# Pooled attention and token mixer: exponentials stored in pairs, value halves split over three matmuls, 22 heads with a column of ones

## Chip, cores and metric

One core of a Trainium2 chip runs the whole program. The metric is device time in microseconds (us) of one execution, from the median of several runs. The engines are TensorE (PE for its matmuls, PEld for its weight loads), VectorE (DVE), ScalarE (ACT), GpSimd (POOL) and SyncE (SP), which issues the transfers.

## What is computed

The input q, k, v has 4 batches of 8 heads, 1152 rows and 64 columns in float32. Attention comes first, with pairs of query rows averaged (576 queries); the heads are then put side by side (512 columns), and a mixer follows over the tokens and over the channels.

```python
q_pool = q.reshape(B, H, S // 2, 2, D).mean(axis=3)
scores = scale * np.matmul(q_pool, k.transpose(0, 1, 3, 2))
scores = scores - np.max(scores, axis=-1, keepdims=True)
attn = np.exp(scores)
attn = attn / (np.sum(attn, axis=-1, keepdims=True) + 1e-09)
x = heads_side_by_side(np.matmul(attn, v))          # 4 x 576 x 512
h = np.maximum(x.transpose(0, 2, 1) @ w_tok1, 0.0) @ w_tok2
u = x + h.transpose(0, 2, 1)
out = u + np.maximum(u @ w_ch1, 0.0) @ w_ch2
```

The mixer's weights come as float64 words and are made float32 on the chip. (The line with heads_side_by_side stands for a transpose and a reshape.)

## The kernel before

Every float32 number that goes into a matmul is split into a high half (rounded to the fast matmul type fp32r) and a low half (the rest), so a product takes two or three fp32r matmuls. The program is a list of steps, each with an engine, an estimated cost and a due time from the table DUE (in units of one step of the attention loop). Plan.run walks through the list and always takes the step that can start first by these estimates, the due time only deciding between equals. What comes out is a fixed order for each engine; on the chip the engines run these orders with semaphores, so a step that takes longer than its estimate delays what stands behind it on its engine.

The 32 heads follow each other (h in main, L757). A head has nine steps s (NK is 9), and each step handles two blocks of 128 keys by 288 queries: the four score matmuls (L781) go into one of two PSUM buffers "s"; ScalarE takes the exponentials of them twice, once in float32 into PF (L791, pf) and once rounded into ph (L794); the difference pl is made by GpSimd or VectorE (L798; both() leaves the choice to the planner, but the first four heads use GpSimd alone). The product with V (L823) adds up in the single PSUM buffer "o" over nine key blocks and is copied out by ScalarE into OT (L828) twice a head, for queries 0 to 287 and 288 to 575. V lies in VV as 64 columns of high half and 64 of low half (L638, L641).

The sum of the exponentials is made in one of two ways. In the heads of IN_PV (18 of 32) one column of VV is set to ones (L645), so that the matmuls of L823 give the sum as one more row; the column that is lost is kept in V0 (L643) and costs a third matmul with weights of one column. In the other 14 heads VectorE adds up the nine blocks of PF (L805), in three pieces of 96 queries for each half of the queries, six a head; the nine numbers that are added lie 288 elements apart.

finish (L832) turns the result to queries by columns and adds the two halves in one go: five plain float32 matmuls of OT with FOLD, two stacked identities (L845). In the 14 heads without ones, five more with a single column of ones add SUM over the partitions (L852). Then come the sum plus a small number (L857), its reciprocal (L859) and the product into U (L864, L867).

Ahead of a head's scores its row maxima are found by matmuls into a ring of three PSUM banks "r" (L717), each reduced by VectorE (L719). The ring also serves the transposes (L575, L601, the mixer's L991), finish and the token mixer (L898, L916). The token weights are narrowed from float64 words (L352 to L362, L513, L521, L523) in the second head, between the attention's steps; their temporaries lie in SBUF. The channel part (L1013, L1041) runs after all heads.

## Time and profile before

| | us |
|---|---|
| median of 3 runs | 947.64 |
| the three runs | 947.71, 941.20, 947.64 |
| span of the profiled execution (first to last instruction) | 940.4 |
| PE busy | 912.0 (97%) |
| PE weight loads busy | 837.5 (89%) |
| VectorE busy | 686.0 (73%) |
| ScalarE busy | 515.1 (55%) |
| GpSimd busy | 377.4 (40%) |
| mean granted TensorE clock | 0.990 |

The profiled execution's span is 0.8 us under the quickest of the timed runs; what lies around the span is thus taken as 0.8 us. The shares are means over the span: attention with the token mixer fills about the first 625 us, and the channel part the rest. The busy time of a matmul in the profile is its latency and overlaps with that of the next; the rate of a stream of matmuls is read from the chain that ended last, where each has only the time that it adds.

### The profile page before, as it was taken

What the parts mean: (1) busy time and instruction counts of PE and PEld (TensorE: products, weight loads), DVE (VectorE), ACT (ScalarE), POOL (GpSimd) and SP (SyncE); (2) the same over time, 40 slices, a digit from 0 to 9 for tenths busy, and PEclk for the clock granted to TensorE, in tenths of its full rate; (3) what the DMA queues carried; (4) which work ended last, traced back from release to release, by engine and by line L of the source; (5) the groups of instructions that cost most, each with busy time, mean ns of one, the idle gap of its engine ahead of it and who ended that gap; (6) DMA issues with size and microseconds to landing.
All of it is one profiled execution on the core that took longest, in us unless ns stands there. A gap on an engine that the chain in (4) does not pass through costs nothing.

```text
span 940.4 us, 15866 instructions
## 1 busy us (share of the span) xinstructions
PE 912.0 (97%) x5857; PEld 837.5 (89%) x5857; DVE 686.0 (73%) x1243; ACT 515.1 (55%) x1040; POOL 377.4 (40%) x342
## 2 busy tenths in 40 slices
PE   7999989999999999999999999999999999999997
PEld 5878879899999989899899999989999998999996
DVE  7887989899999999999999998998872222121311
ACT  3867857687787776776877776854431111111110
POOL 2788866576475574484664763400000000000000
PEclk9999979999999999999999999999999999999999
DMA  6984544537637536645564342034420101000001
GB/s 159 257 184 118 132 105 120 135 87 160 131 86 163 119 86 136 131 113 121 109 138 108 89 108 77 24 97 149 135 90 1 68 1 35 1 34 1 33 1 34
DMA packets 89685, 91.10 MB, mean 97 GB/s; under 512 B 43852, under 2 KB 68808, under 8 KB 89608
## 3 DMA queue, kind: packets, MB, share of 16 engines
q1 hardware_dynamic: 89608, 90.09, 40.4%
q8 instruction: 46, 0.75, 0.4%
q14 instruction: 31, 0.25, 0.1%
HBM read 43.25 MB, written 4.72 MB: 51 GB/s over the span
## 4 chain that ended last, share of the span: by engine, by line
PE 66%; DVE 2%; ACT 1%; DMA 0%; issue 0%; POOL 0%; DVEq 0%; POOLq 0%
PE r L1013 16%; PE s L1041 12%; PE o L823 11%; PE s L781 9%; PE r L717 4%; PE o L1041 3%; PE r L916 3%; PE r L845 2%; PE r L898 2%; PE r L852 1%; PE r L1041 1%; PE r L575 1%; PE r L991 1%; DVE mx L719 1%; DVE pl L798 1%; DMA vn<-in_v_dram 0%
## 5 line engine op out<-in xcount | busy, mean ns | idle before, releaser
L798 POOL TENSOR_TENSOR pl<-pf,ph 128x576 fp32r<-128x576 f32 x194 | 278.4, 1455 | 126.3 <-ACT ph L794 76.1
L791 ACT ACTIVATE pf<-s 128x576 f32<-128x576 f32 x288 | 189.1, 658 | 108.2 <-PE s L781 103.2
L719 DVE TENSOR_REDUCE mx<-r 128x1 f32<-128x384 f32 x384 | 198.4, 548 | 17.1 <-PE r L717 14.5
L794 ACT ACTIVATE ph<-s 128x576 fp32r<-128x576 f32 x288 | 188.9, 657 | 10.3 <-PE s L781 6.4
L781 PE MATMUL s<-qq,kk 128*128 128x288 f32 x574 | 167.6, 304 | 2.9 <-ACT ph L794 2.2
L781 PE MATMUL s<-q,k 65*128 65x288 f32 x576 | 165.5, 300 | 0.5 <-DMA q<-mt 0.2
L1021 DVE SCALAR_TENSOR_TENSOR h<-r,h 128x384 fp32r<-128x384 f32 x72 | 40.1, 556 | 166.9 <-ACT h L1019 166.9
L805 DVE TENSOR_REDUCE sum<-pf 128x96 f32<-128x864 f32 x84 | 146.4, 1750 | 0.2
L823 PE MATMUL o<-ph,vv 128*128 128x288 f32 x576 | 141.5, 306 | 0.2
L1019 ACT ACTIVATE h<-r 128x384 fp32r<-128x384 f32 x72 | 35.3, 491 | 193.5 <-PE r L1013 193.5
L717 PE MATMUL r<-kk,qq 128*128 128x384 f32 x372 | 127.7, 362 | 11.2 <-DVE mx L719 5.2
L823 PE MATMUL o<-pl,vv 128*128 128x288 f32 x576 | 135.5, 299 | 0.5 <-DVE pl L798 0.5
L1041 PE MATMUL s<-w,h 128*128 128x512 f32 x504 | 131.0, 394 | 0.0
L781 PEld LDWEIGHTS s<-qq,kk 128*128 128x128 f32 x574 | 109.4, 191 | 6.9 <-ACT ph L794 5.4
L781 PEld LDWEIGHTS s<-q,k 65*128 65x128 f32 x576 | 110.1, 191 | 1.6 <-issue 1.5
L1013 PE MATMUL r<-big,w 128*128 128x384 f32 x576 | 109.0, 337 | 0.0
L1041 PEld LDWEIGHTS s<-w,h 128*128 128x128 f32 x504 | 93.4, 188 | 16.6 <-DVE h L1021 0.2
L823 PEld LDWEIGHTS o<-pl,vv 128*128 128x128 f32 x576 | 98.2, 190 | 8.4 <-DVE pl L798 0.7
L1013 PEld LDWEIGHTS r<-big,w 128*128 128x128 f32 x576 | 101.8, 188 | 3.9 <-DVE h L1021 0.2
L823 PEld LDWEIGHTS o<-ph,vv 128*128 128x128 f32 x576 | 100.6, 192 | 2.9 <-ACT ot L828 2.1
L717 PEld LDWEIGHTS r<-kk,qq 128*128 128x128 f32 x372 | 69.8, 194 | 20.7 <-DVE mx L719 8.7
L798 DVE TENSOR_TENSOR pl<-pf,ph 128x576 fp32r<-128x576 f32 x94 | 76.6, 819 | 3.9 <-ACT ph L794 3.4
(134 smaller groups left out, 1273.4 us busy)
## 6 DMA issues: line engine op xcount, KB each, us to landing
raw<-in_moe_w_ch_dram SPq DMA_DIRECT2D x24, 512.0 KB
kk<-kh SPq DMA_DIRECT2D x32, 288.0 KB
kk<-kl SPq DMA_DIRECT2D x32, 288.0 KB
qq<-qh SPq DMA_DIRECT2D x64, 144.0 KB
vn<-in_v_dram SPq DMA_DIRECT2D x32, 288.0 KB
k<-kk SPq DMA_DIRECT2D x31, 288.0 KB
kn<-in_k_dram SPq DMA_DIRECT2D x30, 288.0 KB
qn<-in_q_dram SPq DMA_DIRECT2D x32, 256.0 KB
```

Source lines behind the costliest of these rows:

```text
L717: step(PE, mm(SP3), lambda ps=ps, w=w, x=x: te.matmul(at(ps)[:, 0:SP3], w, x, start=True, stop=True), t, read, [ps], [ps])
L719: step(DVE, dve(SP3), lambda ps=ps, m=m: ve.tensor_reduce(m, at(ps)[:, 0:SP3], axis=AX.X, op=ALU.max), t + due["max_of"], [ps], [key])
L781: te.matmul(at(st)[:, i, 0:HF], w[:, c * P:(c + 1) * P], x[:, fq * HF:(fq + 1) * HF], start=(n == 0), stop=(n == len(terms) - 1))
L791: step(ACT, act_ps(2 * HF), lambda pf=pf, st=st: sc.activation(pf, at(st)[:, :, 0:HF], AF.Exp, scale=ESC), t, [(st, 0), (st, 1)], [("pf", s)])
L794: step(ACT, act_ps(2 * HF), lambda ph=ph, st=st: sc.activation(at(ph), at(st)[:, :, 0:HF], AF.Exp, scale=ESC), t + due["p_hi"], [(st, 0), ...
L798: both(2 * HF, lambda e, pf=pf, ph=ph, pl=pl: e.tensor_sub(at(pl), pf, f(at(ph))), t + due["p_lo"], [("pf", s), ph], [pl], [pl], on=POOL i ...
L805: step(DVE, 65 + 1.83 * NK * HF // CUT, lambda fq=fq, cs=cs: ve.tensor_reduce(SUM[:, fq, cs], PF[:, fq * NK:(fq + 1) * NK, cs].rearrange(" ...
L823: lambda o=o, x=x, w=w, m=m, i=i, c=c, new=new, end=end: te.matmul(at(o)[0:m], w[:, c], at(x)[:, i], start=new, stop=end),
L1013: te.matmul(at(ps)[:, 0:GT], w[:, c], x[:, c], start=(c == 0 and n == 0), stop=(c == NC4 - 1 and n == 2))
L1019: step(ACT, act_ps(GT), lambda: sc.activation(at(h)[:, 0], at(ps)[:, 0:GT], AF.Relu), t, [ps], [h])
L1021: step(DVE, dve(GT), lambda: ve.scalar_tensor_tensor(out=at(h)[:, 1], in0=at(ps)[:, 0:GT], scalar=0.0, in1=f(at(h))[:, 0], op0=ALU.max, op ...
L1041: te.matmul(at(ps), a[:, x * P:(x + 1) * P], w, start=(fi == 0 and m == 0), stop=(fi == NF - 1 and m == 2))
```

## The change

- IN_PV grows from 18 to 22 heads, so 10 heads are left in which VectorE adds up the exponentials.
- VV gets 130 columns a block, with a lasting column of ones behind the second half. In the heads of IN_PV the low half of V comes first and the high half second, beside the ones. Three matmuls a block stay: ph with high half and ones (65 columns of weights), ph with the low half (64), pl with high half and ones (65), all into the same rows of "o". V0 and GpSimd's two small steps (L643, L645) go. OT then has 65 rows, with the two halves of V added already.
- In the other heads the two matmuls of 128 columns stay; ScalarE copies the lower rows of "o" to LOW, and VectorE adds them to the upper rows into OT. So "o" is free only after both.
- PF holds neighbouring blocks in pairs: the exponentials of a step are written with a step of two elements (8 bytes), read so by L798, and summed as ten blocks in five pairs, the tenth being zero.
- finish transposes OT (64 or 65 rows by 128 columns) instead of multiplying by FOLD. In the 10 heads without ones, SUM is transposed too (five of 128 by 128) into a second bank of the ring, and VectorE reduces it along the free axis (512 and 128 elements).
- The bits of the token weights are put together in a bank of the ring "r" in place of an SBUF temporary, and the low half is always made by VectorE.
- All numbers of DUE are new, and so the order on every engine can change. The estimate of GpSimd's cost rises a little, and the planner gives VectorE a step that both could do only when GpSimd would end 135 ns later (before 7.7).

```diff
-    "sum": -2.82,
+    "sum": -6.47,
...
-    "stay": 7.7,
+    "stay": 135.0,
...
+IN_PV = (0, 1, 2, 3, 4, 5, 7, 9, 11, 12, 13, 15, 16, 18, 19, 21, 22, 23, 25, 27, 28, 31)
...
-    IN_PV = (0, 1, 2, 3, *range(5, 32, 2))
...
-    FOLDS = 114
+    DT = D + 1
...
-        return 150 + 2.1 * n
+        return 175 + 2.1 * n
...
-    PF = fix.tile([P, 2 * NK, HF], F32, name="pf")
+    PF = fix.tile([P, 2, (NK + 1) // 2, HF, 2], F32, name="pf")
     SUM = fix.tile([P, 2, HF], F32, name="sum")
     REST = words(SUM).rearrange("p f x -> p (f x)")[:, 0:2 * J]
 
 
-    FOLD = many(fix, 2, [P, D + 1], F32, "fold")
+    LOW = fix.tile([D, SQ], F32, name="low")
...
-    VV = many(fix, 2, [P, NK, 2 * D], F32R, "vv")
-    V0 = many(fix, 2, [P, NK, 1], F32R, "v0")
+    VV = many(fix, 2, [P, NK, 2 * D + 2], F32R, "vv")
...
+    for i in range(2):
+        po.memset(f(VV[i])[:, :, P:P + 1], 1.0)
+        po.memset(OT[i], 0.0)
     ve.memset(f(QD[1]), 0.0)
+    po.memset(PF[:, :, NK // 2, :, 1], 0.0)
...
-                w, read = Buf("w"), [("raw", i, c), ("stage",), *(rest if (i, c) == (1, 4) else [])]
+                w, ps, read = Buf("w"), Buf("r"), [
+                    ("raw", i, c), ("stage",), *(rest if (i, c) == (1, 4) else [])]
 
                 def tmp(w=w, r=r, m=m):
                     return at(w)[r, 0:m]
 
-                def clamp(tmp=tmp):
-                    po.tensor_scalar(
-                        out=tmp(), in0=tmp(), scalar1=F64_LEAST, scalar2=F64_MOST,
-                        op0=ALU.max, op1=ALU.min)
-
-                for n, (eng, cost, fn) in enumerate(narrow(tmp, lambda w=words_[r, o]: w, m)):
-                    if n == 1:
-                        eng, cost, fn = POOL, 150 + 1.1 * m, clamp
-                    step(eng, cost, fn, t, read, [w], [w] if n == 0 else [], shared=eng == DVE)
-                step(ACT, act(m), lambda a=wh[r, o], w=tmp: sc.copy(a, w()), t,
-                     [w], [("w", i, c)])
-                both(m, lambda e, a=wl[r, o], w=tmp, d=f(wh)[r, o]: e.tensor_sub(a, w(), d), t,
-                     [w, ("w", i, c)], [("w", i, c)])
+                def low(ps=ps, r=r, m=m):
+                    return at(ps)[r, 0:m]
+
+                def raw_(k, words_=words_, r=r, o=o):
+                    return words_[r, o][:, :, k]
+
+                step(ACT, act(m), lambda raw_=raw_, tmp=tmp: sc.activation(
+                    tmp(), raw_(1).bitcast(F32), AF.Abs), t, read, [w], [w])
+                step(POOL, 150 + 1.1 * m, lambda tmp=tmp: po.tensor_scalar(
+                    out=tmp(), in0=tmp(), scalar1=F64_LEAST, scalar2=F64_MOST,
+                    op0=ALU.max, op1=ALU.min), t, [w], [w])
+                t2 = t + due["w_bits"]
+                step(DVE, dve(m), lambda tmp=tmp, low=low: ve.tensor_scalar(
+                    out=words(low()), in0=words(tmp()), scalar1=0x07FFFFFF, scalar2=3,
+                    op0=ALU.bitwise_and, op1=ALU.logical_shift_left), t2, [w], [ps], [ps])
+                step(DVE, dve(m), lambda raw_=raw_, low=low: ve.scalar_tensor_tensor(
+                    out=words(low()), in0=raw_(1), scalar=0xC0000000, in1=words(low()),
+                    op0=ALU.bitwise_and, op1=ALU.bitwise_or), t2, read, [ps])
+                step(DVE, dve(m), lambda raw_=raw_, low=low: ve.scalar_tensor_tensor(
+                    out=words(low()), in0=raw_(0), scalar=29, in1=words(low()),
+                    op0=ALU.logical_shift_right, op1=ALU.bitwise_or), t2, read, [ps])
+                step(ACT, act_ps(m), lambda a=wh[r, o], low=low: sc.copy(a, low()), t2,
+                     [ps], [("w", i, c)])
+                step(DVE, dve(m), lambda a=wl[r, o], low=low, d=f(wh)[r, o]: ve.tensor_sub(
+                    a, low(), d), t2, [ps, ("w", i, c)], [("w", i, c)])
                 if i == 1 and c == 4:
-                    step(ACT, act(m), lambda a=wh[0:REM, o], w=tmp: sc.copy(a, w()), t,
-                         [w], [("w", i, c)])
+                    step(ACT, act_ps(m), lambda a=wh[0:REM, o], low=low: sc.copy(a, low()), t2,
+                         [ps], [("w", i, c)])
...
-        step(ACT, act(NK * D), lambda: sc.copy(vv[:, :, 0:D], vn),
+        hi, lo = (slice(x, x + D) for x in ((D, 0) if h in IN_PV else (0, D)))
+        step(ACT, act(NK * D), lambda: sc.copy(vv[:, :, hi], vn),
              t, ["vn"], [("vv", h % 2)])
         t += due["v_lo"]
-        both(NK * D, lambda e: e.tensor_sub(vv[:, :, D:2 * D], vn, f(vv)[:, :, 0:D]), t, ["vn", ("vv", h % 2)], [("vv", h % 2)])
-        if h in IN_PV:
-            step(POOL, pool_(NK), lambda: po.tensor_copy(V0[h % 2], vv[:, :, D:D + 1]),
-                 t, [("vv", h % 2)], [("v0", h % 2)])
-            step(POOL, pool_(NK), lambda: po.memset(f(vv)[:, :, D:D + 1], 1.0),
-                 t, [("v0", h % 2)], [("vv", h % 2)])
+        both(NK * D, lambda e: e.tensor_sub(vv[:, :, lo], vn, f(vv)[:, :, hi]), t, ["vn", ("vv", h % 2)], [("vv", h % 2)])
...
-            pf = PF[:, 2 * s:2 * s + 2]
+            pf = (PF[:, 0, s].rearrange("p x i -> p i x") if s < NK // 2
+                  else PF[:, :, NK // 2, :, 0] if s == NK // 2
+                  else PF[:, 1, s - NK // 2 - 1].rearrange("p x i -> p i x"))
...
-                    step(DVE, 65 + 1.83 * NK * HF // CUT, lambda fq=fq, cs=cs: ve.tensor_reduce(
+                    step(DVE, 65 + 1.06 * (NK + 1) * HF // CUT, lambda fq=fq, cs=cs: ve.tensor_reduce(
                         SUM[:, fq, cs],
-                        PF[:, fq * NK:(fq + 1) * NK, cs].rearrange("p c x -> p x c"),
-                        axis=AX.X, op=ALU.add), t + due["sum"] + y * due["sum_each"],
+                        PF[:, fq, :, cs].rearrange("p c x i -> p x c i"),
+                        axis=AX.XY, op=ALU.add), t + due["sum"] + y * due["sum_each"],
                         [("pf", x) for x in range(fq * 4, fq * 4 + 5)], [("sum", fq, y)])
             for i, (fq, c) in enumerate(units):
                 if c == 0:
                     o, parts = Buf("o"), []
-                terms = [(ph, VV[i2], P), (pl, VV[i2], P)]
+                terms = [(ph, 0, P), (pl, 0, P)]
                 if pv:
-                    terms.insert(1, (ph, V0[i2], 1))
+                    terms = [(ph, D, P + 1), (ph, 0, D), (pl, D, P + 1)]
                 for n, (x, w, m) in enumerate(terms):
                     new, end = not parts, (c, n) == (NK - 1, len(terms) - 1)
                     key = (o, "new") if new else (o, c, n)
-                    read = [x, ("v0" if m == 1 else "vv", i2)]
+                    read = [x, ("vv", i2)]
                     if not new:
                         read += parts if end else parts[:1]
                     step(PE, mm(HF),
                          lambda o=o, x=x, w=w, m=m, i=i, c=c, new=new, end=end: te.matmul(
-                             at(o)[0:m], w[:, c], at(x)[:, i], start=new, stop=end),
-                         t + due["pv"] + (x is pl) * due["pv_lo"] + (m == 1) * due["pv_one"], read, [key], [o] if new else [])
+                             at(o)[0:m - w], VV[i2][:, c, w:m], at(x)[:, i], start=new, stop=end),
+                         t + due["pv"] + (x is pl) * due["pv_lo"] + (m == D) * due["pv_one"], read, [key], [o] if new else [])
                     parts.append(key)
                 if c == NK - 1:
-                    step(ACT, act_ps(HF), lambda o=o, fq=fq: sc.copy(
-                        OT[i2][:, fq * HF:(fq + 1) * HF], at(o)), t + due["o"],
-                        parts, [("ot", i2, fq)])
+                    qs = slice(fq * HF, (fq + 1) * HF)
+                    if pv:
+                        step(ACT, act_ps(HF), lambda o=o, qs=qs: sc.copy(
+                            OT[i2][0:DT, qs], at(o)[0:DT]), t + due["o"],
+                            parts, [("ot", i2, fq)])
+                        continue
+                    step(ACT, 415, lambda o=o, qs=qs: sc.copy(
+                        LOW[:, qs], at(o)[D:P]), t + due["o"], parts, [("low", fq)])
+                    step(DVE, 380, lambda o=o, qs=qs: ve.tensor_add(
+                        OT[i2][0:D, qs], at(o)[0:D], LOW[:, qs]), t + due["o"],
+                        [*parts, ("low", fq)], [("ot", i2, fq)])
...
-        ot, den, rd, fold = OT[i2], DEN[i2], RD[i2], FOLD[pv]
+        ot, den, rd = OT[i2], DEN[i2], RD[i2]
         sums = SUM.rearrange("p f x -> p (f x)")
-        n, ps = D + int(pv), Buf("r")
+        ps, part, DS = Buf("r"), Buf("r"), DT + 1
         def turned():
-            return at(ps)[:, 0:NQ * (D + 1)].rearrange("p (c x) -> p c x", c=NQ)
-
+            return at(ps)[:, 0:NQ * DS].rearrange("p (c x) -> p c x", c=NQ)
+
+        def parts(c):
+            return (at(part)[:, c * P:(c + 1) * P] if c < 4
+                    else at(ps)[:, NQ * DS:NQ * DS + P])
+
+        def total():
+            return at(ps)[:, 512 - NQ:512].rearrange("p (c x) -> p c x", x=1)
+
+        n = DT if pv else D
         for c in range(NQ):
-            step(PE, FOLDS, lambda c=c: te.matmul(
-                turned()[:, c, 0:n], ot[:, qc(c)], fold[:, 0:n], start=True, stop=True),
+            step(PE, 64, lambda c=c: te.transpose(
+                turned()[:, c, 0:n], ot[0:n, qc(c)], ident[0:n, 0:n]),
                 t + due["finish_each"] * (c > 3), [("ot", i2, 0), ("ot", i2, 1)], [(ps, 0, c)],
                 [ps] if c == 0 else [])
         keys = [(ps, 0, c) for c in range(NQ)]
         if not pv:
             for c in range(NQ):
-                step(PE, 112, lambda c=c: te.matmul(
-                    turned()[:, c, D:D + 1], sums[:, qc(c)], ones,
-                    start=True, stop=True), t + due["den_sum"], 
-                     [*[("sum", y, z) for y in range(2) for z in range(CUT)], keys[0]], [(ps, 1, c)])
-            keys += [(ps, 1, c) for c in range(NQ)]
-        step(DVE, 70, lambda: ve.tensor_scalar_add(den, turned()[:, :, D:D + 1], EPS),
-             t + due["den"], keys, [("den", i2)])
+                x = ps if c == 4 else part
+                step(PE, TURN, lambda c=c: te.transpose(parts(c), sums[:, qc(c)], ident),
+                     t + due["den_sum"],
+                     [*[("sum", y, z) for y in range(2) for z in range(CUT)], keys[0]], [(x, 1, c)],
+                     [part] if c == 0 else [])
+            step(DVE, dve(4 * P), lambda: ve.tensor_reduce(
+                total()[:, 0:4], at(part).rearrange("p (c x) -> p c x", c=4), axis=AX.X, op=ALU.add),
+                t + due["den"], [(part, 1, c) for c in range(4)], [("rs", 0)])
+            step(DVE, dve(P), lambda: ve.tensor_reduce(
+                total()[:, 4], parts(4), axis=AX.X, op=ALU.add),
+                t + due["den"], [(ps, 1, 4)], [("rs", 1)])
+        den_of = keys if pv else [("rs", 0), ("rs", 1)]
+        step(DVE, 70, lambda: ve.tensor_scalar_add(
+            den, turned()[:, :, D:DT] if pv else total(), EPS),
+             t + due["den"], den_of, [("den", i2)])
```

## Rows read from the trace of the kernel before

**Rows 1.** Busy us by stretch (instructions in brackets), granted clock, DMA; from the windows view.

```profile
core 0: us, PE busy (x) PEld busy (x) DVE busy (x) ACT busy (x) POOL busy (x), PEclk, DMA share, GB/s
20.00:100.00 80.00, 73.72 (x504) 66.35 (x505) 64.74 (x128) 59.48 (x124) 65.12 (x58) 0.98 0.75 176
100.00:150.00 50.00, 44.28 (x263) 38.76 (x261) 44.53 (x73) 33.66 (x71) 31.28 (x29) 0.86 0.55 126
150.00:600.00 450.00, 442.37 (x3251) 417.03 (x3250) 419.69 (x730) 334.20 (x672) 275.79 (x243) 1.00 0.52 114
625.00:940.40 315.40, 310.32 (x1598) 280.91 (x1596) 117.12 (x217) 66.53 (x132) 0.00 (x0) 1.00 0.15 47
```

**Rows 2.** Line L717, what ended PE's idle time before it: us, times.

```profile
  DVE mx L719: 15.0, 29
```

**Rows 3.** Timeline of VectorE at 114 to 122 us: start, length, instructions merged.

```profile
114.60 1.72 DVE L805 TENSOR_REDUCE sum<-pf 128x96 f32<-128x864 f32 x1
117.19 1.69 DVE L805 TENSOR_REDUCE sum<-pf 128x96 f32<-128x864 f32 x1
118.81 0.99 DVE L719 TENSOR_REDUCE mx<-r 128x1 f32<-128x384 f32 x2
119.74 1.61 DVE L805 TENSOR_REDUCE sum<-pf 128x96 f32<-128x864 f32 x1
```

**Rows 4.** Timeline of PE in that stretch; in square brackets the idle time before.

```profile
116.84 0.44 PE L717 MATMUL r<-kk,qq 128*128 128x384 f32 x1 [0.54 <-DVE mx L719]
119.40 1.15 PE L717 MATMUL r<-kk,qq 128*128 128x384 f32 x2 [0.86 <-DVE mx L719]
121.87 0.69 PE L717 MATMUL r<-kk,qq 128*128 128x384 f32 x1 [1.32 <-DVE mx L719]
```

**Rows 5.** The chain that ended last, in order of time: start, us added, instructions.

```profile
285.11 1.06 PE r L852 x10
...
289.74 0.80 PE o L823 x6
...
303.71 1.06 PE r L845 x10
...
768.42 0.98 PE r L991 x9
```

**Rows 6.** Groups by shape on PE: count, busy us, mean ns, idle before.

```profile
L845 PE MATMUL r<-fold,ot 128*128 128x65 f32 x180 | 22.3, 271 | 0.0
L845 PE MATMUL r<-fold,ot 128*128 128x64 f32 x140 | 20.7, 282 | 0.9 <-DVE mx L719 0.9
L852 PE MATMUL r<-ones,sum 128*128 128x1 f32 x140 | 17.3, 248 | 0.0
```

**Rows 7.** Groups by shape on VectorE: reductions and additions.

```profile
L719 DVE TENSOR_REDUCE mx<-r 128x1 f32<-128x384 f32 x384 | 198.4, 548 | 17.1 <-PE r L717 14.5
L805 DVE TENSOR_REDUCE sum<-pf 128x96 f32<-128x864 f32 x84 | 146.4, 1750 | 0.2
L926 DVE TENSOR_TENSOR u<-r,u 128x256 f32<-128x256 f32 x32 | 13.2, 418 | 1.9 <-PE r L916 1.6
L1055 DVE TENSOR_TENSOR raw<-s,u 128x512 f32<-128x512 f32 x13 | 8.5, 683 | 1.5 <-PE s L1041 1.5
```

**Rows 8.** Groups by shape on VectorE: input in steps of 8 bytes, and without steps.

```profile
L359 DVE SCALAR_TENSOR_TENSOR v<-raw,v 128x512 uint32<-128x512 uint32 x24 | 16.5, 687 | 0.3
L976 DVE TENSOR_TENSOR w<-v,w 128x512 fp32r<-128x512 f32 x23 | 15.8, 687 | 4.6 <-ACT w L975 4.6
```

**Rows 9.** Groups by shape around PF and "o" on ScalarE and GpSimd.

```profile
L791 ACT ACTIVATE pf<-s 128x576 f32<-128x576 f32 x288 | 189.1, 658 | 108.2 <-PE s L781 103.2 <-DVE sum L805 1.7
L798 POOL TENSOR_TENSOR pl<-pf,ph 128x576 fp32r<-128x576 f32 x194 | 278.4, 1455 | 126.3 <-ACT ph L794 76.1 <-PE o L823 30.2 <-DVE pl L798 6.9
L828 ACT COPY ot<-o 128x288 f32<-128x288 f32 x64 | 25.8, 403 | 2.1 <-PE o L823 1.7
```

**Rows 10.** Waits of the weight loads on the copy of "o": us, times, longest.

```profile
PEld o L823 <- ACT ot L828: 2.1, 9, 0.3
```

**Rows 11.** Groups by shape on VectorE: bits of the token weights, from SBUF temporaries.

```profile
L359 DVE SCALAR_TENSOR_TENSOR w<-u,w 128x256 uint32<-128x256 uint32 x4 | 4.0, 998 | 0.0
L356 DVE TENSOR_SCALAR w<-w 64x256 uint32<-64x256 uint32 x1 | 2.9, 2872 | 0.0
```

More of the change, by code (lines that the diff above doesn't have):

```diff
@@ L81 @@
-    "mix_1": 2.88,
-    "mix_t": 2.15,
-    "mix_2": 2.85,
-    "mix_u": -93.8,
-    "w_ch": 254.03,
-    "w_ch_each": -79.11,
-    "ut_0": -0.58,
-    "ut_1": -54.13,
-    "stay": 7.7,
+    "scores": -1.44,
+    "p_lo": 1.22,
+    "sum": -6.47,
+    "pv": 2.05,
+    "o": -15.19,
+    "finish": 7.6,
+    "max": -29.13,
+    "max_each": 0.09,
+    "prep": -32.24,
+    "v": 5.77,
+    "stack": 7.14,
+    "stack_2": 14.79,
+    "mix": 9.79,
+    "mix_x": 5.86,
+    "w_tok": 0.59,
+    "w_tok_each": 7.04,
@@ new lines @@
+    "w_bits": -43.21,
+    "sum_each": 2.0,
+    "pv_lo": -0.75,
+    "lo_first": 70.21,
+    "max_first": 50.9,
+    "max_second": 0.54,
+    "scores_each": -12.27,
+    "p_hi": 0.25,
+    "pv_one": -0.26,
+    "finish_each": -35.22,
+    "den_sum": -68.64,
+    "x_lo": 7.7,
+    "x": 8.02,
+    "den": -16.32,
+    "rd": -25.43,
+    "u": -61.47,
+    "u_each": 32.06,
+    "max_of": 6.21,
+    "max_row": -89.36,
+    "max_first_each": 23.6,
+    "q_pool": -42.98,
+    "q_turn": 1.33,
+    "k_each": 2.83,
@@ L403 @@
     early = pool(0, "early", "right")
-    ones = fix.tile([P, 1], F32, name="ones")
-    ve.memset(ones, 1.0)
     KK = many(fix, 3, [P, S], F32R, "kk")
```

72 lines of the change are left out of this document (20 added, 52 removed).

## Prediction

> **What bounds the kernel now.** I read the busy time by stretch first. Between 150 and 600 us PE is busy 442.4 of 450 us (98%), VectorE 419.7 (93%), ScalarE 334.2 (74%), GpSimd 275.8 (61%) [rows 1]. In the channel part from 625 us PE is busy 310.3 of 315.4 us and VectorE little; the change leaves its work as it is. So PE is the bound nearly throughout, with VectorE close behind in the attention. Second, the waits: of the idle time before the maxima's matmuls (L717) VectorE's reductions of earlier maxima end 15.0 us, in 29 places [rows 2]. Third, the timeline shows how such a wait comes about: at 114 to 121 us VectorE runs three sum pieces (L805) of 1.61 to 1.72 us with two maxima between each [rows 3], and in the same stretch PE sits idle 0.54, 0.86 and 1.32 us until a maximum frees a bank of the ring [rows 4]. Some of what looks busy there is waiting too: two matmuls of 384 columns take 1.15 us. Last, the clock: 0.86 of full speed in the mean from 100 to 150 us, 0.98 from 20 to 100, and 1.00 from 150 to 600 [rows 1]. The granted clock has two levels, 1.2 and 2.4 GHz, so this is full-speed work lost of 0.14 x 50 = 7.0 and 0.02 x 80 = 1.6 us. PE had just been idle for several gaps before it.
>
> Two things can thus save time: less work on PE, one for one, and shorter waits behind VectorE.
>
> **PE's work, by terms.** What each matmul adds is read from the chain.
>
> Four more heads with ones: 18 blocks each get a third matmul of 288 columns. Six of L823 add 0.80 us, so 0.133 each [rows 5]; 72 x 0.133 = **+9.6 us**. In the 18 heads that had three matmuls a block there are still three of 288 columns, so nothing changes there; the narrower weights are loaded under the stream.
>
> finish, first half: before, L845 stands with 180 + 140 = 320 matmul records for 32 x 5 calls [rows 6], so each call is two passes, and ten passes add 1.06 us [rows 5]: 32 x 1.06 = 33.9 us. After, 160 transposes. Two prices are possible. The code counts 64 ns, half of a transpose of 128 columns, since only 64 or 65 columns of the identity stream by. But L852 streams a single column and its ten passes still add 1.06 us, 0.106 each [rows 5, 6]: there the weights of 128 columns set the pace, and the new transposes keep 128 columns of weights. Nine transposes of 128 by 128 add 0.98 us, 0.109 each [rows 5]. I take 0.109: 160 x 0.109 = 17.4, **-16.5 us**; by 64 ns it would be 10.2, and -23.7. The Trainium skill, "TensorE: Matmul & The Clock Gate", section "LDWEIGHTS (loading the stationary operand)", speaks against the code's price: a load costs by its columns, the rows don't count. By its columns / 1.2 the estimate is 107 ns for each and 17.1 us for all; L852's rows agree with it for 128 rows, and no row shows a load of 64 rows in this type.
>
> finish, second half: 14 x 1.06 = 14.8 us of L852 go [rows 5, 6]; 10 x 5 transposes of 128 by 128 come, 50 x 0.109 = 5.5. **-9.4 us.**
>
> Sum on PE: 9.6 - 16.5 - 9.4 = **-16.3 us** (-23.5 at the cheap transposes). Since PE is 98% busy, this comes off the span.
>
> **VectorE's work.** A reduction of 384 neighbouring elements takes 548 ns; from 256 to 512 elements an addition grows by 683 - 418 = 265 ns, 1.035 ns an element, so the fixed part of the reduction is 548 - 397 = 151 ns. The sum piece of 864 elements, 288 apart, took 1750, so 1.85 ns an element [rows 7]. In pairs, 960 elements at 1.035 make 994 + 151 = 1.145 us if the pair removes the surcharge, and 1.93 us at 1.85 if it removes nothing. I take the lower: an input in steps of 8 bytes costs VectorE nothing, 687 ns for 512 elements as without steps [rows 8], and two neighbours ask less than that. So 84 x 1.75 = 147 us become 60 x 1.145 = 68.7: -78. New are two reductions in 10 heads, 0.151 + 512 x 0.001035 = 0.68 and 0.28 us, +9.6; and 20 additions of the halves, 288 elements, 418 + 32 x 1.035 = 451 ns, +9.0. Together **-59 us** of the 64.7 + 44.5 + 419.7 = 529 us from 20 to 600 us [rows 1], from 91% to about 84% of a stretch that is 16 us shorter. At the high price of the sum it would be -12.
>
> The token weights' bits have one SBUF input less while GpSimd works: one of these steps took 2.87 us and four a mean of 998 ns [rows 11], where an unhindered one of twice the elements takes 687 [rows 8]. Gain some us of VectorE between 95 and 150 us, where PE waits most. In exchange each of nine pieces holds one of three ring banks for some five steps. I count both at zero; PE has the scores to do meanwhile.
>
> What this is worth to the span: the waits of 15.0 us come with pieces of 1.7 us, 84 of them. With 1.15 us and 60 the blocked time is less than half; some of the waits are from the start, before any sum. I take 6 us (bounds 0 and 12). Of the 7.0 us that the clock costs around 120 to 150 us I take half, **3.5** (0 to 7), as the gaps ahead of it were sum pieces [rows 3, 4].
>
> **ScalarE, GpSimd.** The exponentials are written in steps of 8 bytes. No row shows such a write. Below, it costs nothing (658 ns [rows 9]); above, it pays VectorE's surcharge for far steps, 1.85 - 1.035 = 0.82 ns an element, +0.47 us x 288 = 135 us, which would lift ScalarE from 427 to 562 us of the 580 from 20 to 600 us [rows 1]. I take nothing, since 8 bytes are nearer to the reading of rows 8 than to 1152 bytes. The Trainium skill, "SBUF — State Buffer", section "Door 1: The DMA port swizzle", has SBUF lines of 16 bytes, with full rate at two hits to a line: by it the surcharge is zero, and the -16.3 stands; no run here shows it for a write. GpSimd reads PF in the same steps; at 61% busy [rows 1] it has cover, except in the first four heads, which use it alone: 9 x 1.46 = 13.1 us a head [rows 9] against some 18 us that a head takes ((600 - 20) / 32), so up to 0.5 us more on each is hidden. The two small steps of prep_v go, off the path.
>
> "o": the copy of 403 ns is now followed by an addition of 451 ns in 10 heads, 20 times. PE's loads wait on the copy 2.1 us in all, 0.3 at most [rows 10], so the copy is well covered now. Uncovered, the addition costs 20 x 0.45 = 9 us; I take 0 for the forecast, 9 for the upper bound. Queued behind it: on VectorE the next maxima and differences; on PE the next head half's product.
>
> **Sum.** 940.4 - 16.3 - 6 - 3.5 = 914.6 us of span, and 0.8 around it makes 915.4. The profiled execution is of the kind of the quickest run (941.2); the other two took 6.5 us more, for a reason no row shows. The changed kernel gets half of this, 3 us, for its median: **918 us**.
>
> **Rivals.**
> 1. *Cheap transposes.* 64 ns each: 7.2 us less, 911. For it: only 64 columns stream; against it: L852. Chance 0.14.
> 2. *The pair doesn't help the sum.* 1.93 us a piece: VectorE keeps nearly its load, the waits stay. Only PE's -16.3 comes: 924.1 + 0.8 + 3 = 928. For it: pairs still jump 2304 bytes between each two. Chance 0.10.
> 3. *The strided write costs ScalarE.* At 562 us of work in a stretch of about 560, ScalarE sets the pace; with the 20 us that starting and ending the stretch take that is 582 us in place of 580, and 940.4 + 2 + 0.8 + 3 = 946. Chance 0.06. With it I count 0.07 for a new order whose own waits eat the gain, 940 to 950: every due time is new, and estimates and chip differ (114 ns against 212 for a call of L845).
> 4. *The other side: "o" waits in VectorE's queue.* The addition is behind what the fixed order has put ahead of it. The first half of the queries ends in the same step of the loop in which three sum pieces are due; two pieces ahead cost 2 x 1.145 + 0.451 = 2.74 us, 20 times 55 us: 918 + 55 = 973. It decides from about 1.5 us a time (30 us), when the gain is gone. Against it: PE still has two score buffers to fill, and the addition can be placed ahead of the pieces. Chance 0.11, of which the milder cases end near 960.
>
> **How the numbers follow.** The forecast has 0.52, and ends between 906 and 931: lower with 12 us of waits and all 7 of the clock gone and no spread (940.4 - 16.3 - 12 - 7 + 0.8 = 906); higher with no relief of either kind and the whole spread (940.4 - 16.3 + 0.8 + 6.5 = 931). The range for 8 in 10 takes in rival 1 with these reliefs, 906 - 7 = 899, and at the top the addition of 9 us uncovered, 940. A measurement can tell about 1%, 9.5 us here. Faster by over 1% (under 938): forecast, rivals 1 and 2 less a little, 0.74. Within 1%: rival 3, the new order and the edge of the others, 0.15. Slower: rival 4, 0.11.
>
> **What would show it.** Sum pieces near 1.15 us, 60 of them; five single transposes in finish adding 0.55 us a head (0.32 by rival 1); 72 more matmuls of 288 columns in L823's groups; the exponentials into PF still near 658 ns; VectorE's share from 150 us on at about 85%; the waits of L717 on VectorE's maxima under 10 us; the clock from 100 to 150 us above 0.9. I am wrong if PE shows new waits on the addition into OT or on ring banks, if the exponentials into PF rise above about 0.9 us, or if the sum of idle time and lost clock in the attention grows by more than the 16 us that PE's work shrinks.

## The result and the profile after

The changed kernel takes 931.12 us (median of 4 runs, 930.03 to 935.47). Against runs of the kernel before on the same chip that is 0.9856 of its time (95% interval 0.9812 to 0.9900). It is faster, but by 1.4% where 3.1% was forecast, 13 us above the 918 of the forecast and within its range of 899 to 940. Span against span, as the sum was made, 940.4 became 929.8: 10.6 us less, not 25.8.

The page of the changed kernel, busy time first:

```profile
span 929.8 us, 15513 instructions
PE 883.9 (95%) x5679; PEld 817.7 (88%) x5679; DVE 635.0 (68%) x1291; ACT 520.4 (56%) x1040; POOL 331.6 (36%) x273
```

PE's busy time fell by 912.0 - 883.9 = 28.1 us, more than the forecast asked for. But its idle time, span less busy, rose from 28.4 to 45.9, by 17.5 us; 28.1 - 17.5 is the gain of 10.6. The windows view shows where (columns as in [rows 1]):

```profile
20.00:100.00 80.00, 74.75 (x505) 67.09 (x506) 59.34 (x139) 62.89 (x134) 68.76 (x53) 0.98 0.80 187
100.00:150.00 50.00, 45.80 (x325) 43.42 (x324) 41.82 (x88) 39.14 (x78) 27.46 (x23) 0.97 0.58 131
150.00:600.00 450.00, 423.91 (x3096) 402.59 (x3095) 385.90 (x781) 337.22 (x668) 221.12 (x176) 1.00 0.48 111
```

From 150 to 600 us PE is idle 26.1 us, where it was 7.6 [rows 1], while VectorE went from 93% to 86% busy and the granted clock from 100 to 150 us from 0.86 to 0.97. What PE waits for stands in the list of its waits (engine, what waited, for what: us, times, longest), of the changed kernel:

```profile
PE r L726 <- DMA kk<-kl: 26.0, 19, 2.6
PE s L791 <- ACT ph L806: 3.3, 10, 0.5
PE r L726 <- DVE mx L728: 2.1, 4, 1.0
```

L726 is the maxima's matmul (L717 before), and kk<-kl the transfer that puts the low half of a head's keys below the high half. The same two waits in the kernel before:

```profile
PE r L717 <- DVE mx L719: 5.2, 9, 1.3
PE r L717 <- DMA kk<-kl: 2.2, 1, 2.2
```

Rows 2 are from another view, that of one line, which adds up the idle time ahead of its matmuls and ahead of their weight loads; the 15.0 us there are thus not PE's matmuls alone. After, this view of L726 has (us, times):

```profile
  DMA kk<-kl: 29.4, 21
  DVE mx L728: 8.1, 17
```

So the wait behind VectorE's maxima about halved, from 15.0 to 8.1 us with the weight loads [rows 2] and from 5.2 to 2.1 us without them, and a wait for a transfer that was hardly there took its place. One instance, from the chain that ended last, from SP's timeline and from PE's (in square brackets the idle time before):

```profile
277.12 0.31 PE r L873 x5
...
284.27 4.39 DMA kk<-kl
288.65 0.14 issue
288.79 0.41 PE r L726
```

```profile
279.24 0.87 SPq L701 DMA_DIRECT2D q<-mt  x1
280.16 0.60 SPq L704 DMA_DIRECT2D q<-mt  x1
280.81 0.58 SPq L671 DMA_DIRECT2D k<-kk  x1
281.44 0.59 SPq L674 DMA_DIRECT2D q<-ql  x1
282.08 1.45 SPq L666 DMA_DIRECT2D qq<-qh  x2
283.63 0.54 SPq L666 DMA_DIRECT2D kk<-kh  x1
284.27 0.54 SPq L666 DMA_DIRECT2D kk<-kl  x1
```

```profile
288.79 0.41 PE L726 MATMUL r<-kk,qq 128*128 128x384 f32 x1 [1.61 <-DMA kk<-kl]
```

VectorE had the last third of the low key half ready at 279.35 us; seven transfers of the same queue go out first, at some 0.6 us each, which the planner counts (650 ns). Then this one takes 4.4 us from issue to landing, and PE, with the first maximum next in its order, sits idle for 1.6 us until then. The planner has it landing 1400 ns after issue, plus its bytes (288 KB at 360 bytes a ns, 0.82 us), plus 900: 3.1 us, a little more when the transfer ahead is still under way. The 18 such transfers in the chain took 4.07 to 5.98 us, 4.9 in the median.

The plans of the two kernels show what changed, worked out with Plan.run from their own estimates. In the plan of the kernel before, the first matmul that reads this transfer's tile stands over 1 us behind the planned landing in 27 of 32 heads, in the median 6.8 us. In the plan of the changed kernel it stands within 0.3 us of it in 23 of 32.

### The profile page after: what moved, and what is told of

Same layout as the page of the kernel before. It is cut to its first block, busy times and chain, and to the rows that moved or that the text cites. A ratio compares the mean times of both kernels' runs of the same rounds, so it can differ in the third digit from the quotient of the medians.

```text
span 929.8 us, 15513 instructions
## 1 busy us (share of the span) xinstructions
PE 883.9 (95%) x5679; PEld 817.7 (88%) x5679; DVE 635.0 (68%) x1291; ACT 520.4 (56%) x1040; POOL 331.6 (36%) x273
## 4 chain that ended last, share of the span: by engine, by line
PE 71%; DMA 10%; ACT 7%; DVE 6%; SPq 4%; issue 2%; DVEq 0%; ACTq 0%; POOL 0%; POOLq 0%
PE r L1049 16%; PE o L835 13%; PE s L1077 13%; PE s L791 11%; DMA kk<-kl 10%; PE r L726 7%; PE o L1077 3%; ACT pf L803 3%; ACT ph L806 2%; SPq L666 2%; DVE mx L728 2%; PE r L934 2%; PE r L588 1%; PE r L952 1%; PE r L1077 1%
## 5 line engine op out<-in xcount | busy, mean ns | idle before, releaser
L810 POOL TENSOR_TENSOR pl<-pf,ph 128x576 fp32r<-128x576 f32 x170 | 245.4, 1459 | 189.0 <-ACT ph L806 94.0
L803 ACT ACTIVATE pf<-s 128x576 f32<-128x576 f32 x288 | 201.2, 700 | 121.3 <-PE s L791 115.5
L835 PE MATMUL o<-ph,vv 128*64 128x288 f32 (+2 forms) x972 | 211.5, 299 | 1.2 <-ACT ot L842 1.1
L728 DVE TENSOR_REDUCE mx<-r 128x1 f32<-128x384 f32 x384 | 189.2, 547 | 29.7 <-PE r L726 28.8
L791 PE MATMUL s<-qq,kk 128*128 128x288 f32 x574 | 169.4, 306 | 3.4 <-ACT ph L806 3.3
L791 PE MATMUL s<-q,k 65*128 65x288 f32 x576 | 166.2, 299 | 0.2 <-ACT q L760 0.2
L726 PE MATMUL r<-kk,qq 128*128 128x384 f32 x372 | 124.8, 352 | 30.5 <-DMA kk<-kl 26.0
L835 PEld LDWEIGHTS o<-ph,vv 128*64 128x64 f32 (+2 forms) x972 | 136.5, 146 | 6.4 <-ACT ot L842 2.2
L835 PE MATMUL o<-pl,vv 128*65 128x288 f32 (+1 forms) x576 | 140.0, 300 | 0.8 <-POOL pl L810 0.5
L791 PEld LDWEIGHTS s<-qq,kk 128*128 128x128 f32 x574 | 109.9, 192 | 9.0 <-ACT ph L806 6.9
L791 PEld LDWEIGHTS s<-q,k 65*128 65x128 f32 x576 | 110.6, 192 | 0.5 <-ACT q L760 0.5
L810 DVE TENSOR_TENSOR pl<-pf,ph 128x576 fp32r<-128x576 f32 x118 | 92.7, 787 | 24.5 <-ACT ph L806 19.5
L1077 PEld LDWEIGHTS s<-w,h 128*128 128x128 f32 x504 | 93.4, 188 | 16.6
L726 PEld LDWEIGHTS r<-kk,qq 128*128 128x128 f32 x372 | 69.6, 192 | 39.6 <-issue 23.3
L835 PEld LDWEIGHTS o<-pl,vv 128*65 128x65 f32 (+1 forms) x576 | 83.4, 153 | 3.9 <-POOL pl L810 1.8
L817 DVE TENSOR_REDUCE sum<-pf 128x96 f32<-128x960 f32 x60 | 67.7, 1138 | 0.8 <-ACT pf L803 0.4
```

What stands on the lines that cost most here:

```text
L726: step(PE, mm(SP3), lambda ps=ps, w=w, x=x: te.matmul(at(ps)[:, 0:SP3], w, x, start=True, stop=True), t, read, [ps], [ps])
L728: step(DVE, dve(SP3), lambda ps=ps, m=m: ve.tensor_reduce(m, at(ps)[:, 0:SP3], axis=AX.X, op=ALU.max), t + due["max_of"], [ps], [key])
L791: te.matmul(at(st)[:, i, 0:HF], w[:, c * P:(c + 1) * P], x[:, fq * HF:(fq + 1) * HF], start=(n == 0), stop=(n == len(terms) - 1))
L803: step(ACT, act_ps(2 * HF), lambda pf=pf, st=st: sc.activation(pf, at(st)[:, :, 0:HF], AF.Exp, scale=ESC), t, [(st, 0), (st, 1)], [("pf", s)])
L810: both(2 * HF, lambda e, pf=pf, ph=ph, pl=pl: e.tensor_sub(at(pl), pf, f(at(ph))), t + due["p_lo"], [("pf", s), ph], [pl], [pl], on=POOL i ...
L817: step(DVE, 65 + 1.06 * (NK + 1) * HF // CUT, lambda fq=fq, cs=cs: ve.tensor_reduce(SUM[:, fq, cs], PF[:, fq, :, cs].rearrange("p c x i -> ...
```

## The experiments

Each is compared with the kernel before on the same chip; the brackets hold the 95% interval of the ratio. Differences between two experiments, or to the changed kernel, are of medians that mostly come from different chips, on which the medians of the kernel before were 942.89 to 947.67 us.

**The landing in the plan, later by 1.2 us, what the quicker of these transfers lack.**

```diff
-                s.end = wire + 900
+                s.end = wire + 2100
```

> The changed kernel, with one number of the planner altered: a transfer is taken to land 2100 ns after its bytes are through, not 900 (in the changed kernel's trace the copies of the low key halves into KK took 4.3 us from issue to landing, the plan has 3.1). All work stays, only the orders change. Theory A (the gain went into a new wait: the order puts the first maxima right where the plan has the key halves landing, and PE then idles about 1.2 us a head, 26 us in all): the wait of the maxima's matmuls for that transfer falls from 26 to under 8 us, and the time to 905 to 918. Rival B (the chain keys, transfer, maxima, scores is what a head takes, whatever the order): the wait turns up at the scores or at another transfer, and the time stays at 925 to 937.

Measured: 918.44 us, ratio 0.9721 (0.9688 to 0.9754), 12.7 us less than the changed kernel. PE's wait for the key halves in it:

```profile
PE r L726 <- DMA kk<-kl: 6.5, 10, 1.4
```

26.0 us became 6.5, as theory A says; the time just misses its 905 to 918. But every order was made anew, so by itself this is not proof; three more runs show how much a new order alone can do. First, 3300 in that line (late24):

> late12 with the landing at 3300 ns behind the bytes, 1.2 us later than what was measured. Theory A (the order only has to keep up with the real landing): the wait for the key halves falls below 3 us, and the time stays within 5 us of late12, 913 to 923. Rival F (a later landing in the plan lengthens the chain of each head): 924 or more.

Measured: 939.29 us, 0.9964 (0.9939 to 0.9989). The wait went as expected, the time did not; what ended idle time before L726 there (matmuls and weight loads):

```profile
  DVE mx L728: 26.9, 50
  DMA kk<-kl: 1.2, 2
```

Rival F holds as to the time. Two things go with it: the waits for VectorE grew (the first of these lines has 8.5 us in late12), and the granted clock is 0.982 in the mean of the runs, where late12 has 0.996. That alone is 0.014 x 940 = 13 us of the 20.9 between the two; what lowered the clock isn't shown. Then 2100 in the kernel before:

> The kernel before with the planner's landing of transfers set to 2100 ns behind the bytes, as in late12; no work changes. Theory A (the wait for the key halves is a matter of the new order constants: before, that transfer made PE wait 2.2 us only, so there is little to mend): within 6 us of before, 937 to 949. Rival E (the landing estimate costs every order some 13 us, and the change's own worth is thus only 17 us): 928 to 936.

Measured: 956.24 us, 1.0139 (1.0098 to 1.0179): no gain, as A said, but slower by more than A's 6 us; that its due times fit the old estimate is a guess. And in late12 the due times searched anew with the kernel's own planner, 54 of its constants, the exponentials into PF now counted at 45 ns more each; two of them and that line:

```diff
-    "max_second": 0.54,
+    "max_second": -71.15,
...
-    "k_lo": 37.53,
+    "k_lo": 0.34,
...
-            step(ACT, act_ps(2 * HF), lambda pf=pf, st=st: sc.activation(
+            step(ACT, act_ps(2 * HF) + 45, lambda pf=pf, st=st: sc.activation(
```

> The changed kernel with the landing at 2100 ns as in late12, 45 ns more for the exponentials into PF (700 against 655 ns), and due times searched anew by the planner's own estimates; no work altered. Theory A (with the landing right, PE's work and the waits that the order leaves are what counts): the key halves' wait stays under 8 us and the time falls below late12, 905 to 915. Rival F (an order's time on the chip scatters by 10 us whatever the plan says): anywhere from 910 to 930.

Measured: 923.93 us, 0.9786 (0.9743 to 0.9830), 5.5 us above late12, though the planner's own end for it lay 8.8 us lower (with the 45 ns counted in both); PE waited 6.8 us for the key halves. Some 5 of the 5.5 us can be the granted clock, 0.990 against 0.996 in the mean. Theory A's 905 to 915 is missed, rival F holds: three orders of the same work, late12, tuned and late24, lie at 918, 924 and 939 us. The plan has the wrong sign for tuned; for late24 it has the right one, an end 16.4 us behind late12's.

**Two parts undone, with new orders.** The 18 old heads in late12:

> late12 with the 18 heads with ones of the kernel before in place of 22. PE has 72 matmuls of 0.133 us less (9.6) but 20 transposes more (2.2); VectorE has 24 sum pieces of 1.14, and 4 heads' additions and reductions more, some 35 us. Theory A (PE's work counts one for one as long as no transfer is waited for): 7 us less than late12, 909 to 914. Rival C (VectorE's load decides): 4 or more us longer than late12, above 922.

Measured: 924.48 us, 0.9798 (0.9765 to 0.9831). The exponentials as before in late12 (PF of 18 blocks, L817 over nine far blocks):

> late12 with the exponentials stored as before (blocks 288 elements apart, no pairs, no tenth block): a sum piece takes 1.75 us in place of 1.14, 60 times, so VectorE has 37 us more; the exponentials' write is without steps and should take 658 ns again, not 700. Theory A (VectorE's relief is worth little where PE is the bound, as in before_sum): within 4 us of late12, 914 to 923. Rival D' (the pair carries the gain): 10 or more us longer, above 928.

Measured: 927.20 us, 0.9822 (0.9791 to 0.9854). Both are slower than late12, by 6.0 and 8.8 us, against theory A in both; far_late12 ends between the bounds of its two theories. It speaks for VectorE's load counting in these orders, but both differences are of the size by which new orders scatter, so neither part's worth is settled.

**The wait taken away in the changed kernel's own orders.** These leave the plan as it is. A first try read 64 rows:

```diff
-                w, x = QQ[i3][:, qc(c)], KK[i3][:, ks]
+                hr = slice(j * D, (j + 1) * D)
+                w, x = QHI[p % 2][hr, qc(c)], KHI[hr, ks]
```

> The changed kernel in its own orders, every engine's unaltered. Only the maxima's matmuls of heads 1 to 31 read the high halves of queries and keys straight from the tiles that the transposes fill (64 rows; the low half's share of the row maxima is left out), so they wait for no transfer; matmuls and columns are as many as before. Theory A (PE's idle time for the key halves' transfer, 26 us, is what the gain went into): the wait is gone, 10 to 24 us less than the changed kernel, 907 to 921. Rival B (the scores need the same transfer a little later, so the wait moves there): within 4 us of the changed kernel, 927 to 935.

> The same edit in the kernel before, in its own orders: the maxima's matmuls read the high halves from the source tiles (the low half's share of the maxima is left out). Theory A: PE waits 2.2 us for that transfer here, so within 5 us of before, 938 to 948. Rival B' (the wait was hidden in what looked busy): 10 or more us less, under 934.

Measured: 1044.46 us, 1.1061 (1.0971 to 1.1152), and 1075.77, 1.1407 (1.1360 to 1.1453). Neither theory had this. Nothing waits for a transfer there; the matmul itself got slow, as the timeline of PE shows for the changed kernel (start, length):

```profile
300.96 0.44 PE L727 MATMUL r<-kh,qh 64*128 64x384 f32 x1
301.33 0.35 PE L836 MATMUL o<-ph,vv 128*64 128x288 f32 x1
301.61 0.44 PE L727 MATMUL r<-kh,qh 64*128 64x384 f32 x1
```

The next matmul starts 0.37 us after it; 384 columns at 128 rows add 0.17 to 0.18. The matmul of 288 columns ahead of it takes longer too, 0.28 us here (301.33 to 301.61) and 0.22 in the median, where 0.13 is usual. So these two runs say nothing about the wait, and the edit was replaced by one that keeps the old shape:

```diff
-                w, x = QQ[i3][:, qc(c)], KK[i3][:, ks]
+                w, x = QHI[p % 2][:, qc(c)], KHI[:, ks]
```

> The changed kernel in its own orders. The maxima's matmuls of heads 1 to 31 read the high halves of a pair of heads, 128 rows, straight from the tiles that the transposes fill (the maxima are then those of the two heads' scores added, a shift that the softmax takes out again), so they wait for no transfer; shape and count of the matmuls stay as in the changed kernel. Theory A (PE's idle time for that transfer, 26 us, is what the gain went into): 10 to 24 us less than the changed kernel, 907 to 921. Rival B (the scores need the same transfer a little later, so the wait moves there): within 4 us of the changed kernel, 927 to 935.

Measured: 908.02 us, 0.9622 (0.9587 to 0.9658), 23.1 us less than the changed kernel. PE's waits in it, the two longest:

```profile
PE s L791 <- ACT ph L806: 7.9, 10, 3.2
PE r L726 <- DVE mx L728: 4.6, 3, 3.7
```

The orders are the changed kernel's, the shapes too, no wait for a transfer is left, and the gain is nearly the 26.0 us of the wait; some 7 us came back as longer waits for ScalarE and VectorE (3.3 and 2.1 us in the changed kernel). Theory A holds, rival B falls.

> The same edit in the kernel before, in its own orders. Theory A: PE waits 2.2 us for that transfer here, so within 6 us of before, 937 to 948. Rival B' (the wait was hidden in what looked busy): 10 or more us less, under 934.

Measured: 942.46 us, 0.9987 (0.9965 to 1.0008). Before, that wait cost nothing that can be measured; it is the change's own.

**PE's and VectorE's work, taken away in the kernel before, in its own orders.** Single transposes in finish:

```diff
-            step(PE, FOLDS, lambda c=c: te.matmul(
-                turned()[:, c, 0:n], ot[:, qc(c)], fold[:, 0:n], start=True, stop=True),
+            step(PE, FOLDS, lambda c=c: te.transpose(
+                turned()[:, c, 0:n], ot[0:n, qc(c)], ident[0:n, 0:n]),
```

> The kernel before in its own order, with only the matmuls with FOLD replaced by single transposes of the upper 64 or 65 rows (the low halves of V are left out of the result). At 61 ns each, as the changed kernel's trace shows, PE has 33.9 - 9.8 = 24 us less to do. Theory A (PE's work comes off the span one for one, as predicted): 24 us less than before, 920 to 927 against 947. Rival C (with VectorE at 93% PE's saved time is spent waiting for VectorE): under 10 us less, above 937.

Measured: 938.45 us, 0.9923 (0.9886 to 0.9960): about 7 us by the ratio, 5 by the medians. But PE did not have 24 us less to do. In the 14 heads without ones the transposes have 64 rows, and what stands around them got slower. The chain around such a head, first before, then before_turn:

```profile
284.77 0.18 PE r L717
...
285.11 1.06 PE r L852 x10
286.17 0.95 PE r L845 x8
287.12 0.23 PE r L717
```

```profile
285.84 0.17 PE r L717
286.01 0.20 PE r L845
286.21 1.21 PE r L852 x10
287.42 0.39 PE r L845 x4
287.81 0.38 PE r L717
```

From the end of the first of these lines to the end of the last it is 2.40 us before and 2.18 after (284.95 to 287.35, 286.01 to 288.19), 0.22 us less. In the 18 heads with ones 1.06 us [rows 5] became 0.31. Together that is 14 x 0.22 + 18 x 0.75 = 16.6, some 17 us in place of 24. PE's waits in before_turn:

```profile
PE r L717 <- DVE mx L719: 6.5, 11, 1.6
PE r L717 <- DMA q<-mt: 5.8, 4, 2.7
PE r L717 <- DMA kk<-kl: 4.8, 3, 2.3
```

All its waits for transfers rose from 3.6 to 11.9 us, while that for maxima rose only from 5.2 to 6.5. The granted clock fell from 0.990 to 0.987 in the mean of the runs, some 3 us. This is about what is missing of the 17 us. Rival C has the time right but not its reason, as it is mainly transfers that PE waits for. Five blocks in each sum piece:

```diff
-                        PF[:, fq * NK:(fq + 1) * NK, cs].rearrange("p c x -> p x c"),
+                        PF[:, fq * NK:fq * NK + 5, cs].rearrange("p c x -> p x c"),
```

> The kernel before in its own order, each sum piece adding five of its nine blocks (480 elements, far apart; the other four are left out of the sum). A piece should take 151 + 480 x 1.85 = 1.04 us in place of 1.75, so VectorE has 59 us less, as much as forecast for the change. Theory A (the relief takes away the waits behind sum pieces, some 6 us and part of the clock's loss): 5 to 12 us less than before. Rival D (VectorE's load is off PE's path): under 3 us.

Measured: 942.05 us, 0.9995 (0.9970 to 1.0020). VectorE's busy time fell from 686.0 to 632.6 us and the time not at all: rival D. Both together:

> Both of the two edits in the kernel before, in its own order (low halves of V and four of nine blocks of the sum left out). Theory A (independent): the sum of the two, some 30 to 36 us less than before, 911 to 918. Rival C (each alone is held back by the other engine): clearly more than the sum of the two single gains. Rival B (the chain through the transfers is the next bound): less than the sum, with PE waiting for the key halves' transfer as in the changed kernel.

Measured: 934.54 us, 0.9900 (0.9871 to 0.9928), about 9 us: the sum of the two gains as measured, not the 30 to 36 of theory A. And with the maxima read directly as well:

> before_turn_sum (single transposes in finish without the low halves of V, sum pieces of five blocks) with the maxima read from the source tiles as in before_direct, in the orders of the kernel before. Theory A (transfers ate the gain there too: PE waited 6.6 us for them in before_turn_sum): 6 to 12 us less than before_turn_sum, 922 to 928, and PE's waits for transfers under 2 us. Rival H (what ate it is the fixed order of the three engines among themselves, waits of 1 us and less in many places): within 4 us of before_turn_sum, 930 to 937.

Measured: 930.51 us, 0.9870 (0.9840 to 0.9901), 4.0 us less than before_turn_sum, with intervals that overlap. PE's waits in it:

```profile
PE r L717 <- DVE mx L719: 5.3, 8, 1.9
PE s L781 <- ACT ph L794: 4.6, 7, 2.0
PE r L717 <- ACT kh L584: 2.9, 4, 2.1
```

No transfer is left among them, and some 12 of the 17 us are gained. Rival H, short waits of the three engines for each other, has the time right, but it isn't shown to be the rest: PE is idle 927.6 - 897.9 = 29.7 us here and 28.4 before, so what transfers no longer cost turned up as waits for ScalarE (8.2 us in all, 3.3 before), and no more. The granted clock is 0.986 in the mean of the runs against 0.991 before, which makes some 4 of the 5 us that are missing. What lowers it stays open.

**The 64-row shape, and the best version.** Transposes of 65 rows in all heads, in late12 and in after_direct:

```diff
-        n = DT if pv else D
+        n = DT
```

> late12 with the transposes of finish at 65 rows also in the 10 heads without ones, where they had 64. By the changed kernel's trace five transposes of 65 rows add 0.31 us. Theory G (64 rows make a matmul run at half the pace, as with the maxima of 64 rows): the ten heads' transposes, at 0.11 us each in late12, fall to 0.06, 2.5 us less on PE, time 914 to 918. Rival (they are slow for another reason, the transposes of the sums in between): the same pace, and within 1 us of late12.

Measured: 914.10 us, 0.9679 (0.9642 to 0.9716), 4.3 us less than late12. The transposes of finish in a head without ones, and the matmuls between and behind them, from the chain; first the changed kernel (64 rows), then late12_65, where the same instructions happen to follow each other:

```profile
312.28 0.20 PE r L873
312.48 0.26 PE r L881
312.74 0.39 PE r L873 x4
313.13 1.07 PE o L835 x7
```

```profile
306.15 0.12 PE r L873
306.28 0.12 PE r L881
306.39 0.24 PE r L873 x4
306.64 0.93 PE o L835 x7
```

With 64 rows these add 1.92 us, with 65 rows 1.41. It isn't the transposes' own pace, as theory G has it: by the starts of single matmuls in the changed kernel's trace, one transpose of 64 rows follows another after 0.062 us in the median, as one of 65 rows does. What costs is each change between 64 rows and 128. From the last transpose of 64 rows to the next matmul of 128 it takes 0.178 us (0.035 with 65 rows), and a transpose of SUM (L881) ahead of one of 64 rows takes 0.259 us (0.113 ahead of 65 rows, in late12_65). With 0.51 us a head, 10 heads make 5.1 us, near the 4.3 that were gained. Theory G's range for the time held, but its 2.5 us on PE was too small and its mechanism is not the one seen.

> after_direct with the transposes of finish at 65 rows in all heads. Theory G: PE has 50 x 0.05 = 2.5 us less; late12_65 gained 4 us so: 903 to 907. Rival: the time that PE saves is waited for elsewhere, 907 to 910.

Measured: 903.09 us, 0.9575 (0.9549 to 0.9600): the best of all, 4.3% under the kernel before and 4.9 us less than after_direct. Its shift in the softmax is the maximum of two heads' scores added, which cancels; it asks that this sum stay near each head's own maximum, and no run here has other inputs than these.

## Why the prediction was off, step by step

*"Since PE is 98% busy, this comes off the span."* This is the step that failed: the sum takes PE's saving and VectorE's off the span whole and has no term for waits of the new order. In the changed kernel PE's work fell by about 19 us, but its idle time rose by 17.5, as it waits 26.0 us in 19 places for a transfer that it hardly waited for before. In the same orders without this wait (after_direct) the time is 23.1 us less. In the old order, too, PE's saving did not come off whole: before_turn took some 17 us from PE and gained 5 to 7, with 8 us more of waits for transfers and some 3 us of clock. before_all, without waits for transfers and with a lighter VectorE, gained 12. So a busy share of 98% says who is busiest, not that nothing else is close behind; here it was transfers. after_direct, whose VectorE is as busy as that of before_all (635.8 and 636.1 us) but whose order was made for the shorter work, has 35 us less than the kernel before.

*PE's work.* Forecast -16.3 us. From the chain's rows after, 22 heads have 0.31 us for finish's five transposes, 10 have 0.59 (0.20 and 0.39) and for SUM's five another 0.70 (0.26 and 0.44). That is 19.7 us in place of 48.7, and with the 9.6 of the new matmuls PE has about 19 us less. The term that was mis-sized is finish's first half, 12.7 us and not 17.4 (the second half came out at 7.0, not 5.5): I took 0.109 us for a transpose because L852's passes take 0.106 with one column streaming. Here weights of 65 rows and 128 columns go by in 0.062. Rival 1 and the code's 64 ns were right for a transpose between others of its kind; the changes between 64 and 128 rows, in 10 heads, were in neither price. For a weight load the Trainium skill, "TensorE: Matmul & The Clock Gate", section "LDWEIGHTS (loading the stationary operand)", has columns / 1.2, which is 107 ns for 128 columns; the trace's 0.062 us from one of these transposes to the next doesn't go by it.

*VectorE.* The prices held: a sum piece took 1138 ns (forecast 1145), the two reductions 696 and 300 (680 and 280), the addition 446 (451). Two groups of the changed kernel, the sum piece and ScalarE's exponentials into PF:

```profile
L817 DVE TENSOR_REDUCE sum<-pf 128x96 f32<-128x960 f32 x60 | 67.7, 1138 | 0.8 <-ACT pf L803 0.4
L803 ACT ACTIVATE pf<-s 128x576 f32<-128x576 f32 x288 | 201.2, 700 | 121.3 <-PE s L791 115.5 <-DVE sum L817 3.9
```

Rival 2 fell. VectorE gave up 51.0 us of busy time, not 59, since 118 differences pl are its own now, where it had 94. The waits behind its maxima fell by 6.9 us (6 forecast), but the 15.0 us that the forecast took them from hold weight loads too; the matmuls alone waited 5.2 us and now wait 2.1. That this is a gain of its own isn't borne out: before_sum gained nothing. The clock's lost time fell from 9.4 to (1 - 0.993) x 929.8 = 6.5 us, 2.9 (3.5 forecast).

*ScalarE.* The strided write costs 42 ns (700 against 658 ns), 12 us over 288, far under the bound of 470 ns each; ScalarE stays at 75% of 150 to 600 us. In far_late12, with the old layout, it is 654 ns again. The Trainium skill's lines of 16 bytes ("SBUF — State Buffer", "Door 1: The DMA port swizzle") have it at zero; the measured number is small, but not zero. Rival 3's first half fell.

*"o".* L835 waits 1.1 us for the copy in the heads with ones (L842) and not visibly for the addition: the 0 held, rival 4 fell.

*The new order.* I gave 0.07 to "a new order whose own waits eat the gain", as a thing without a place. It was the loss that came, and it had a place that the diff names: the due times of "stack", "stack_2", "max" and "k_lo" all moved, and with them seven queued transfers and PE's first maximum, set by a landing of 3.1 us or little more where 4.1 to 6.0 are measured. What I left out is the term for it: 19 waits of about 1.4 us. None of the signs of being wrong that I named came up, as none was a transfer: idle time and lost clock from 20 to 600 us together grew by some 10 us, not 16. Without this wait the sum would have been near by luck, 909.2 us of span in after_direct against 914.6, from a mixture that was wrong in PE's and in VectorE's term. What lies around the span is 1.8 us (931.58 against 929.8), not the 0.8 that I took.

What stays open: which of the due times brought the wait about, what 22 heads and the pairs are worth apart from the order, and why the granted clock differs between orders.

## What to carry to other kernels

When a schedule is made from estimates, look at each transfer's measured time from issue to landing and compare it with the estimate: work placed right at an estimated landing turns every missing microsecond into idle time of the busiest engine. Work taken from an engine that is 98% busy is gained one for one only if nothing else that it waits for ends just as late; try it in the old order first, and read from the trace how much work was really taken, and whether the granted clock stayed the same. A change that makes a new order should be compared with a few other new orders: three of the same work spread over 21 us here.

## What the hardware showed that was not expected

- Changes between matmuls of 64 rows and of 128 rows cost time on PE. A maximum of 64 rows and 384 columns took 0.37 us to the start of the next matmul of 128 rows, where 128 rows take 0.18, and the matmul of 288 columns ahead of it 0.22 in the median where 0.13 is usual (after_nodma). Around transposes a change adds some 0.14 us, while transposes of 64 rows among themselves are as quick as those of 65, 0.062 us. Two maxima of 64 rows in a row were 0.28 us apart, so there it is not the change alone. Why it costs isn't shown.
- 65 rows between matmuls of 128 rows show no such cost: L791 with 65 rows and 288 columns takes 0.135 us to the next start (changed kernel); of L823, with 128 rows, six add 0.80 us, 0.133 each [rows 5].
- Weights of 65 rows and 128 columns in plain float32 pass every 0.062 us in transposes, where the passes of L852 with 128 rows need 0.106 [rows 5].
